# Decode attention with a gated feed-forward branch: other order of loads, other place of the feed-forward part, shorter output sum

## The chip, the cores and the metric

The kernel runs on one core of a Trainium2 chip. The metric is the device time of one execution in microseconds (us), median of several runs. Before the change it is 390.3 us. The profile's span, from the first to the last instruction, is about 1.8 us shorter than the time of the same run.

Engines: PE is the TensorE matrix engine (PEld its weight loads), DVE the VectorE, ACT the ScalarE, POOL the GpSimd, SP the SyncE, which here only issues DMA transfers. SP and POOL each feed a DMA queue of their own: q1 (hardware) is SP's, q0 (software) is POOL's. The trace of the changed kernel shows it: from 30 to 90 us, when only SP's keys are loaded, q1 moves 24.98 of 25.12 MB, and from 156 to 186 us, when only POOL's values are, q0 moves 12.55 of 12.60 MB.

## The reference

Two sequences (B = 2), one new token each, 32 heads of width 128, 4096 cached keys and values per head, everything in bf16:

```python
x = A_x                                                     # [2, 1, 512]
g = sigmoid((x * gate_w).sum(-1, keepdims=True))
q = (x @ wq).reshape(B, 1, 32, 128).transpose(0, 2, 1, 3)
p = softmax(einsum("bhqd,bhkd->bhqk", q, k_cache) * 128 ** -0.5)
o = einsum("bhqk,bhkd->bhqd", p, v_cache)
a = o.transpose(0, 2, 1, 3).reshape(B, 1, 4096) @ wo        # wo: [4096, 512]
b = relu(x @ w1) @ w2                                       # w1: [512, 1376], w2: [1376, 512]
return g * a + (1 - g) * b
```

The caches are read once: 64 keys and 64 values ("K0" to "K63", "V0" to "V63", one per head and sequence) of 1 MiB each. The weights wq and wo are 4 MiB each, w1 and w2 1.4 MB each. By my estimate from the numbers below (146.1 MB at 420 GB/s are 348 of the 387.6 us of the span) it is a kernel that should run at the speed of its loads.

## The kernel before

For each sequence ("batch" in what follows): load the 32 keys, transpose each on TensorE, multiply by the query; then one softmax over all heads; then the 32 values, in groups of four heads; each group's output goes through its part of wo. Keys have four buffers (KN), transposed keys four (KT), values seven (varena). wq, w1 and w2 lie in the memory of the value buffers, so no value can be loaded before the feed-forward part (FFN) is done. The loads are issued like this (cut):

```python
@block.sync
def _(sp):
    for i in range(NHEAD):                                   # the 64 keys
        s, u = kn_slot(i)
        if i == 0:
            sp.wait_ge(d_w2b, 16)                            # all of w2 has landed
        if u > 0:
            sp.wait_ge(pe_tk[NQ - 1], i - NKN + 1)           # the key four earlier is transposed
        sp.dma_start(out=KN[s], in_=...).then_inc(kn_sem[s], 16)
    sp.wait_ge(dv_out, 3)
    sp.dma_start(out=out..., in_=out_bf[0:1, :]).then_inc(d_out, 16)

@block.gpsimd
def _(pool):
    pool.iota(...); pool.iota(...)
    # x, gate_w, wq, w1, w2 (two parts), wo: all issued here, in this order
    pool.wait_ge(pe_f2, 1)                                   # FFN done: the value buffers are free
    for i in range(NHEAD):                                   # the 64 values
        b, h = divmod(i, Hq)
        s, u = vslot(i)
        if h == 0:
            il = b * Hq + Hq - 1                             # the batch's last key has landed
            ks, ku = kn_slot(il)
            pool.wait_ge(kn_sem[ks], 16 * (ku + 1))
        if u > 0:
            pool.wait_ge(vfree[s], u)                        # the head seven earlier is done
        pool.dma_start(out=VS[s], in_=...).then_inc(vsem[s], 16)
```

TensorE does everything in program order: the query projection, the FFN, then per batch the keys (scores two heads behind the transposes), the softmax transposes, the values. The DVE adds each group's output row to `acc_row` and at the very end forms `(acc - b) * g + b` in three operations over 1x1024 elements on one partition.

## Time and profile before

| | before |
|---|---|
| time, median (lowest to highest) | 390.3 us (389.2 to 391.5) |
| span of the profiled run | 387.6 us |
| bytes moved | 146.1 MB |
| rate in undisturbed stages | 418 to 423 GB/s |
| PE busy | 82% of the span |
| key head: transposes and scores on PE / its DMA at 420 GB/s | 1.94 + 0.55 us / 2.50 us |

These lines of the page are the span, the busy share of the DMA engines in 40 slices of 9.7 us, and what they moved in each slice:

```profile
span 387.6 us, 10707 instructions
...
DMA  4999999999999999999992699999978999999950
GB/s 180 419 344 389 409 419 419 418 420 420 419 398 420 422 419 420 419 421 419 420 419 117 220 413 423 419 419 419 421 316 315 427 419 418 420 420 420 419 221 0
```

146.1 MB at 420 GB/s are 348 us. So 40 us of the span are not explained by bytes, and the GB/s line shows where they are: the first slices, slice 3 (344), slices 22 and 23 (117 and 220), slices 30 and 31 (316 and 315), and the last two.

A finer reading is needed to know what ends each hole. The following lines are of the view by windows. The columns are the window, its length, busy time and number of instructions of PE, PEld, DVE, ACT and POOL, then the granted TensorE clock (1.00 is full speed), the busy share of the DMA engines, and GB/s. First the start:

```profile
0.00:4.00 4.00, 0.00 (x0) 0.00 (x0) 1.72 (x4) 1.28 (x1) 3.36 (x9) 1.00 0.01 1
4.00:8.00 4.00, 0.37 (x8) 0.29 (x8) 2.66 (x4) 0.00 (x0) 4.00 (x5) 1.00 0.78 256
```

Then the place between the batches:

```profile
204.00:208.00 4.00, 3.43 (x59) 3.24 (x60) 0.00 (x0) 0.00 (x0) 0.00 (x0) 1.00 0.54 221
208.00:212.00 4.00, 3.50 (x50) 2.47 (x47) 0.75 (x2) 0.00 (x0) 0.00 (x0) 1.00 0.02 8
212.00:216.00 4.00, 4.00 (x49) 2.75 (x49) 3.33 (x7) 0.02 (x1) 0.00 (x0) 1.00 0.02 4
216.00:220.00 4.00, 4.00 (x72) 3.47 (x69) 4.00 (x7) 2.45 (x3) 0.00 (x0) 1.00 0.76 256
```

TensorE works at full clock all the time while DMA moves next to nothing from 208 to 216 us: the values of batch 0 have all landed, four keys of batch 1 were loaded long ago, the fifth key waits for TensorE to transpose the first, and the first value of batch 1 waits for the last key. That wait is in the list of waits (engine, what it was about to do, what it waited for: us in total, times, longest):

```profile
POOL varena L204 <- DMA kn_arena<-in_A_k_cache_dram: 206.9, 2, 110.5
```

and what it costs is seen when it ends for the second time, at 291 us, just after the last key has landed:

```profile
284.00:288.00 4.00, 3.27 (x53) 2.10 (x50) 2.71 (x5) 2.02 (x2) 0.00 (x0) 1.00 0.98 403
288.00:292.00 4.00, 3.25 (x55) 2.73 (x56) 2.04 (x4) 1.01 (x1) 0.72 (x2) 1.00 0.13 55
292.00:296.00 4.00, 2.74 (x45) 1.46 (x42) 2.72 (x4) 1.01 (x1) 2.94 (x6) 1.00 0.83 301
```

Finally the end, from the chain of waits (start, duration, what, how many instructions): the last value's matmuls, the output projection of the last groups, and then four DVE operations (the 0.69 us sum of the last group and the three of 1.22 us) that nothing overlaps:

```profile
376.42 1.95 PE PS L453 x32
...
379.68 1.83 PE PS L437 x8
...
381.53 0.69 DVE acc_row L318
...
382.31 1.22 DVE t_row L322
...
383.56 1.22 DVE t_row L327
...
384.81 1.21 DVE out_bf L330
```

### The profile page before, as it was taken

What the parts mean: (1) busy time and instruction counts of PE and PEld (TensorE: products, weight loads), DVE (VectorE), ACT (ScalarE), POOL (GpSimd) and SP (SyncE); (2) the same over time, 40 slices, a digit from 0 to 9 for tenths busy, and PEclk for the clock granted to TensorE, in tenths of its full rate; (3) what the DMA queues carried; (4) which work ended last, traced back from release to release, by engine and by line L of the source; (5) the groups of instructions that cost most, each with busy time, mean ns of one, the idle gap of its engine ahead of it and who ended that gap; (6) DMA issues with size and microseconds to landing.
All of it is one profiled execution on the core that took longest, in us unless ns stands there. A gap on an engine that the chain in (4) does not pass through costs nothing.

```text
span 387.6 us, 10707 instructions
## 1 busy us (share of the span) xinstructions
PE 318.7 (82%) x5008; PEld 258.3 (67%) x5008; DVE 165.0 (43%) x280; ACT 74.9 (19%) x80; POOL 41.4 (11%) x77
## 2 busy tenths in 40 slices
PE   0355799999896688987888999999984799988873
PEld 0333677777673677776776877777762799877761
DVE  4023477777677100111111877777766102111106
ACT  1001244443344300000000433344433100000000
POOL 7000000000003022221200000000003032222000
PEclk9998899999999599999999999999998599999998
DMA  4999999999999999999992699999978999999950
GB/s 180 419 344 389 409 419 419 418 420 420 419 398 420 422 419 420 419 421 419 420 419 117 220 413 423 419 419 419 421 316 315 427 419 418 420 420 420 419 221 0
DMA packets 20766, 146.11 MB, mean 377 GB/s; under 512 B 2194, under 2 KB 2194, under 8 KB 3827
## 3 DMA queue, kind: packets, MB, share of 16 engines
q0 software_dynamic: 11504, 78.32, 49.5%
q1 hardware_dynamic: 9218, 67.12, 42.2%
q8 instruction: 39, 0.64, 0.7%
q14 instruction: 5, 0.03, 0.0%
HBM read 145.43 MB, written 0.00 MB: 375 GB/s over the span
## 4 chain that ended last, share of the span: by engine, by line
DMA 46%; PE 45%; DVE 3%; issue 2%; ACT 2%; POOL 1%; POOLq 0%; DVEq 0%
DMA varena<-in_A_v_cache_dram 27%; PE PS L381 25%; DMA kn_arena<-in_A_k_cache_dram 15%; PE PS L453 11%; PE PS L398 6%; DMA varena<-in_B_w_dram 5%; PE PS L437 2%; DVE mx L272 1%; DVE mx L271 1%; ACT P L221 1%; ACT P L219 1%; ACT kt_arena L212 1%; PE PS L427 0%; DVE t_row L327 0%; DVE t_row L322 0%
## 5 line engine op out<-in xcount | busy, mean ns | idle before, releaser
L453 PE MATMUL PS<-varena,pT 128*1 128x128 bf16 x2048 | 127.2, 223 | 20.1 <-DMA varena<-in_A_v_cache_dram 17.8
L381 PEld LDWEIGHTS PS<-iden,kn_arena 128*128 128x128 bf16 x2048 | 116.4, 99 | 38.4 <-DMA kn_arena<-in_A_k_cache_dram 36.7
L269 DVE COPY kt_arena<-PS 128x1024 bf16<-128x1024 bf16 x192 | 120.7, 684 | 45.8 <-PE PS L381 45.8
L453 PEld LDWEIGHTS PS<-varena,pT 128*1 128x1 bf16 x2048 | 118.5, 86 | 30.3 <-DMA varena<-in_A_v_cache_dram 25.7
L381 PE MATMUL PS<-iden,kn_arena 128*128 128x128 bf16 x2048 | 127.2, 221 | 9.8 <-DMA kn_arena<-in_A_k_cache_dram 9.6
L212 ACT COPY kt_arena<-PS 128x1024 bf16<-128x1024 bf16 x64 | 64.8, 1012 | 218.6 <-PE PS L381 218.6
L204 POOL DMA_DIRECT2D varena<-in_A_v_cache_dram x64 | 33.9, 532 | 318.7 <-DMA kn_arena<-in_A_k_cache_dram 206.9
L307 DVE TENSOR_TENSOR osb<-PS,rs_row 1x512 bf16<-1x512 f32 x16 | 10.9, 679 | 133.8 <-PE PS L453 133.8
L398 PE MATMUL PS<-kt_arena,Qm 128*32 128x512 bf16 x512 | 39.0, 384 | 0.4 <-ACT kt_arena L212 0.4
L437 PE MATMUL PS<-wo_sb,OT 128*1 128x512 bf16 x64 | 16.1, 378 | 0.0
L398 PEld LDWEIGHTS PS<-kt_arena,Qm 128*32 128x32 bf16 x512 | 8.0, 94 | 8.0 <-DVE kt_arena L269 1.4
L318 DVE TENSOR_TENSOR acc_row<-acc_row,PS 1x512 f32<-1x512 f32 x16 | 10.8, 675 | 5.8 <-PE PS L437 5.8
L346 PE MATMUL PS<-xT,varena 128*128 128x2 bf16 x128 | 3.6, 165 | 11.6 <-DMA varena<-in_A_wq_dram 11.6
L346 PEld LDWEIGHTS PS<-xT,varena 128*128 128x128 bf16 x128 | 3.5, 104 | 11.7 <-DMA varena<-in_A_wq_dram 11.7
L364 PE MATMUL PS<-varena,h1T 128*1 128x512 bf16 (+1 forms) x22 | 6.6, 468 | 4.1 <-DMA varena<-in_B_w_dram 4.1
L437 PEld LDWEIGHTS PS<-wo_sb,OT 128*1 128x1 bf16 x64 | 4.2, 82 | 5.0 <-DVE OT L313 0.4
L364 PEld LDWEIGHTS PS<-varena,h1T 128*1 128x1 bf16 (+1 forms) x22 | 2.1, 98 | 8.1 <-DMA varena<-in_B_w_dram 4.1
L249 DVE CAST QT<-PS 128x64 bf16<-128x64 f32 x1 | 0.2, 225 | 12.7 <-PE PS L346 12.7
L415 PE MATMUL PS<-iden,P 32*128 32x32 bf16 x64 | 0.9, 187 | 5.4 <-ACT P L221 5.4
L262 DVE COPY b_row<-PS 1x1024 f32<-1x1024 f32 x1 | 1.2, 1212 | 9.2 <-PE PS L364 9.2
L406 PE MATMUL PS<-idenf,mx 128*1 128x128 f32 x2 | 0.6, 322 | 5.2 <-DVE mx L272 5.2
L415 PEld LDWEIGHTS PS<-iden,P 32*128 32x128 bf16 x64 | 0.7, 101 | 5.6 <-ACT P L221 5.6
(58 smaller groups left out, 53.4 us busy)
## 6 DMA issues: line engine op xcount, KB each, us to landing
kn_arena<-in_A_k_cache_dram SPq DMA_DIRECT2D x64, 1024.0 KB, 7.9
varena<-in_A_v_cache_dram POOLq DMA_DIRECT2D x64, 1024.0 KB, 15.1
varena<-in_A_wq_dram POOLq DMA_DIRECT2D x1, 4096.0 KB, 12.8
wo_sb<-in_A_wo_dram POOLq DMA_DIRECT2D x1, 4096.0 KB, 41.5
varena<-in_B_w_dram POOLq DMA_DIRECT2D x1, 1376.0 KB, 15.5
varena<-in_B_w_dram POOLq DMA_DIRECT2D x1, 1280.0 KB, 19.9
varena<-in_B_w_dram POOLq DMA_DIRECT2D x1, 96.0 KB, 19.4
x_row<-in_A_x_dram POOLq DMA_DIRECT2D x1, 2.0 KB, 2.2
```

Source lines behind the costliest of these rows:

```text
L204: pool.dma_start(out=VS[s], in_=src).then_inc(vsem[s], 16)
L212: act.copy(out=KT[kt_slot(i)][:, (NQ - 1) * JQ * 128:NQ * JQ * 128], in_=STG[NQ - 1]).then_inc(ac_kq, 1)
L219: act.activation(out=P[0:64, :], in_=PS[0:64, 0:PW], func=ACT.Exp, bias=negm[0:64, :], scale=SCALE, accum_out=ssum[0:64, 0:1]).then_inc(ac ...
L269: dve.tensor_copy(out=KT[kt_slot(i)][:, q * JQ * 128:(q + 1) * JQ * 128], in_=STG[q]).then_inc(dv_kq, 1)
L307: dve.tensor_tensor(out=osb[0:1, g * 512:(g + 1) * 512].rearrange("o (m d) -> o m d", m=4), in0=PS[0:1, g * 512:(g + 1) * 512].rearrange(" ...
L318: dve.tensor_tensor(out=acc_row[0:1, b * D:(b + 1) * D], in0=acc_row[0:1, b * D:(b + 1) * D], in1=PS[0:1, gbank(g2) * 512:(gbank(g2) + 1) ...
L346: mm = pe.matmul(QT_ps[:, 2 * h:2 * h + 2], lhsT=wq_sb[:, k, h * Dh:(h + 1) * Dh], rhs=xT[:, k, :], start=(k == 0), stop=(k == KD - 1))
L364: mm = pe.matmul(PS[0:1, B_COL + b * D:B_COL + (b + 1) * D], lhsT=h1T[0:fw, u, b:b + 1], rhs=w2_sb[0:fw, u, :], start=(u == 0), stop=(u == ...
L381: t = pe.transpose(out=STG[q][:, (j - q * JQ) * 128:(j - q * JQ + 1) * 128], in_=KN[s][:, j * Dh:(j + 1) * Dh], identity=iden[:, :])
L398: mm = pe.matmul(PS[32 * tcol:32 * tcol + 32, beta * 512:(beta + 1) * 512], lhsT=Qm[:, b, h, :], rhs=kt[:, c * 512:(c + 1) * 512], start=( ...
L437: mm = pe.matmul(PS[0:1, gbank(g) * 512:(gbank(g) + 1) * 512], lhsT=OT[:, b, h:h + 1], rhs=wo_sb[:, h, :], start=(m == 0), stop=(m == 3))
L453: mm = pe.matmul(PS[0:1, col:col + Dh], lhsT=pT[:, j, h:h + 1], rhs=VS[s][:, j * Dh:(j + 1) * Dh], start=(j == 0), stop=(j == NJ - 1))
```

## The change

The intent is to keep DMA busy where it ran dry, and to shorten the end:

1. w1 and w2 get memory of their own (paid for by three KT buffers instead of four and by placing small rows in memory that is free at that time), so values get eight buffers and need not wait for the FFN.
2. SP issues half of wq and then w1 and w2 at the very start; POOL issues the other half of wq before x. Keys wait for wq only.
3. The FFN moves on TensorE and DVE from before the first key to between the softmax and the values of batch 0.
4. wo is loaded after the keys of batch 0, by SP instead of POOL, and K32 and the keys after it are held back until V30 has landed.
5. The values of a batch start when its third key from the end has landed.
6. `(1 - g) * b` is put into `acc_row` once; each group's row is then added as `g * row + acc` in one fused operation, and the last one writes the output.

```diff
-    NKT = 4
-    NADDR_V = 7
+    NKT = 3
+    NADDR_V = 8
+    w1_sb = sb("w1_sb", [128, KD, Dff], BF16)        # were parts of varena
+    w2_sb = sb("w2_sb", [128, NFF, D], BF16)
...
     @block.sync
+        # wq rows of the second half -> d_wq2, then w1, then w2 (two parts)
         for i in range(NHEAD):
+            if b > 0 and h == 0:
+                sp.dma_start(out=wo_sb[:, :, :], in_=A_wo.rearrange("(h p) n -> p h n", p=128)).then_inc(d_wo, 16)
+                vs_, vu_ = vslot(b * Hq - 2)
+                sp.wait_ge(vsem[vs_], 16 * (vu_ + 1))
             if i == 0:
-                sp.wait_ge(d_w2b, 16)
+                sp.wait_ge(d_wq, 16)
+                sp.wait_ge(d_wq2, 16)
...
     @block.gpsimd
-        # x, gate_w, wq, w1, w2, wo
-        pool.wait_ge(pe_f2, 1)
+        # first half of wq, x, gate_w
+        pool.wait_ge(pe_q, 1)
...
-                il = b * Hq + Hq - 1
+                il = b * Hq + Hq - 3
...
     @block.vector
-                    dve.tensor_tensor(out=acc_row[...], in0=acc_row[...], in1=PS[...], op=ALU.add)
-        # t1 = acc - b;  t1 = t1 * g;  out = t1 + b     (1x1024 each)
+                    dst = acc_row if g2 < NG - 1 else out_bf
+                    dve.scalar_tensor_tensor(out=dst[...], in0=PS[...], scalar=g_row[0:1, b:b + 1],
+                                             in1=acc_row[...], op0=ALU.mult, op1=ALU.add)
...
     @block.tensor
-        # query projection, FFN, then the batches
+        # query projection, then the batches; in batch 0 the FFN follows the softmax transposes,
+        # and the values wait until its result is copied out (dv_bcp)
```

## The prediction

> **What bounds it now.** The DMA queues view gives 146.1 MB. In undisturbed stages the windows view shows 418 to 423 GB/s at a DMA share of 1.01, so the bytes alone need about 348 us of the 387.6 us span. A key head takes TensorE 1.94 + 0.55 = 2.49 us in the chain of waits and DMA 1.05 MB / 420 = 2.50 us: balanced. A value head takes TensorE about 2.0 us. The kernel is bound by DMA, and its 40 us above the byte time are holes (windows of 2 us):
> - start: nothing until about 5.4 us; POOL issues everything;
> - 18 to 44 us: 320 to 410 GB/s, about 3 us lost;
> - 205 to 219 us: about 11.5 us lost between the batches. Only four keys of batch 1 are prefetched; the next waits for TensorE, values for the last key;
> - 287 to 293.5 us: about 5 us lost, because batch 1's first value waits until the last key has landed (POOL idle 96 us, ended at 291.3);
> - from the last value's bytes (about 375 us) to the end: 12.6 us, with four DVE operations after the last matmul (0.68 and three of 1.21 us).
>
> **What the change does.** Bytes and matmuls stay the same.
> - SP issues half of wq and the FFN weights at once; I expect data from about 2.2 us: 3 us gained. Keys wait for wq only; the first lands at about 23.5 us instead of 34. Most of that is no gain: wo's 4.2 MB (10 us) only moves to the values of batch 0.
> - K32 to K35 move from early in the values of batch 0 to its end, where DMA was empty; wo takes their old place. The 11.5 us hole shrinks to about 1 us: 10 us gained, the largest term.
> - Values start two keys earlier: the 5 us hole almost closes (4 to 4.5 us), though the last two keys, sharing the engines, land about 2.5 us later.
> - Tail: three 1.21 us operations with gaps (3.8 us) go; the fused one should cost the same 0.68 us.
> - Cost: the FFN (1.6 us + relu + 6.6 us + copy, about 11 us with gaps) now stands between softmax and values of batch 0, partly at the half clock that the trace shows there (0.50). The eighth value slot and wo give DMA 35 us of queued work from the 30th key on, TensorE's pause is about 33 us: 0 to 3 us of new hole.
> - Cost: the first keys meet a half clock (3.6 instead of 1.96 us) with only keys to load: up to 2 us of hole.
>
> [...]
>
> **Sum.** Span 387.6 - 3 - 10 - 4.5 - 3.8 + 2 = 368, less about 2 of the early dip: 366; with the 1.8 us between span and time, 368 us, 5.7% faster. Range 362 to 376. Faster by over 2%: 0.95; within: 0.04; slower: 0.01.
>
> **What would show it.** DMA share near 1.0 through both batch changes; first key transposed near 23.5 us; batch 1's first transpose near 198 us (214 now); one short DVE operation after the last output matmul.
>
> **What would make it wrong.** A hole of over 4 us behind the FFN; keys sharing with values so that the key chain falls behind; TensorE, nearly as long as DMA, becoming the bound.

## The result

| | before | changed |
|---|---|---|
| time, median (lowest to highest, runs) | 390.25 us (389.15 to 391.5, 16) | 370.37 us (369.46 to 372.04, 9) |
| ratio, 95% interval | | 0.950 (0.948 to 0.951) |
| span of the profiled run | 387.6 us | 368.5 us |
| first transpose of a key | 34.3 us | 23.6 us |
| first transpose of batch 1 | 214.0 us | 201.5 us |
| packets of all DMA | 20,766 | 25,133 |

Ratios in this document are the mean time of one kernel's runs over that of the other's of the same rounds, so they are not quite the ratio of the medians. Executions over 1.5% slower than the fastest of the same kernel are left out of the means. The kernel is 5.0% faster.

The same lines of the page, for the changed kernel (a slice is 9.2 us):

```profile
span 368.5 us, 10705 instructions
...
DMA  8999999999999999999998999999999999999990
GB/s 304 397 399 421 422 416 421 419 417 420 397 407 408 392 393 415 419 420 423 416 383 317 421 422 414 420 422 420 419 414 414 419 349 419 422 420 419 421 393 10
```

The DMA line now has a 9 or an 8 in all but the last slice. The GB/s line is the more honest one: slices 11 to 15 (392 to 408), 21 and 22 (383 and 317) and 33 (349) still show losses, some of them under a 9.

The same windows, the start, then the place between the batches, then the second softmax:

```profile
0.00:4.00 4.00, 0.00 (x0) 0.00 (x0) 0.96 (x3) 1.28 (x1) 3.33 (x9) 1.00 0.55 152
4.00:8.00 4.00, 0.00 (x0) 0.00 (x0) 0.00 (x0) 0.00 (x0) 0.00 (x0) 1.00 1.00 422
```

```profile
190.00:194.00 4.00, 3.42 (x59) 3.04 (x55) 0.46 (x1) 0.00 (x0) 0.00 (x0) 1.00 0.74 307
194.00:198.00 4.00, 3.45 (x59) 3.26 (x60) 0.00 (x0) 0.00 (x0) 0.00 (x0) 1.00 0.79 297
198.00:202.00 4.00, 4.00 (x37) 1.90 (x35) 2.68 (x6) 0.00 (x0) 0.00 (x0) 1.00 0.98 336
```

```profile
274.00:278.00 4.00, 4.00 (x67) 2.90 (x65) 2.83 (x6) 2.02 (x2) 3.10 (x6) 1.00 0.98 391
278.00:282.00 4.00, 3.41 (x60) 2.81 (x57) 2.79 (x5) 1.01 (x1) 1.07 (x3) 1.00 1.01 418
296.00:300.00 4.00, 4.00 (x71) 4.00 (x69) 0.00 (x0) 0.00 (x0) 1.06 (x2) 0.95 0.81 299
300.00:304.00 4.00, 4.00 (x76) 4.00 (x73) 0.68 (x1) 0.00 (x0) 1.41 (x3) 1.00 1.02 375
```

And the end of the chain of waits: one fused operation stands after the last matmul (L457 is the output projection, L343 the fused sum).

```profile
361.04 1.95 PE PS L475 x32
...
364.30 1.83 PE PS L457 x8
...
366.16 0.74 DVE Qm L343
```

### A ledger of lost DMA time

To compare the two kernels stage by stage, take windows of 2 us and count in each how much time its bytes did not need at 420 GB/s: 2 us minus GB/s times 2 us over 420. The sum over the span is the span minus 348 us, so every microsecond of difference between the two spans must be in one of the lines. (A stage at a rate slightly over 420 gives a small negative number.)

| stage | before | changed | difference |
|---|---|---|---|
| start, to 18 / 16 us | 5.5 | 2.7 | -2.8 |
| rest of the weights, first keys, to 44 / 24 us | 2.8 | 0.8 | -2.0 |
| rest of the keys of batch 0 | 0.6 | 0.2 | -0.4 |
| values of batch 0 (from 120 / 96 us) | 0.0 | 2.3 | +2.4 |
| between the batches (204 to 220 / 190 to 200) | 11.3 | 3.0 | -8.4 |
| keys of batch 1 | 0.4 | 0.2 | -0.2 |
| around the second softmax (286 to 294 / 274 to 306) | 4.8 | 1.8 | -3.0 |
| values of batch 1 | -0.1 | -0.1 | 0.0 |
| end (from 372 / 358 us) | 14.3 | 9.7 | -4.6 |
| total | 39.7 | 20.5 | -19.1 |

The total is the difference of the spans, 387.6 - 368.5. The largest line is the one that the prediction had as its largest. One line has the wrong sign: the values of batch 0 lose 2.3 us that they did not lose before. (The last keys of batch 0 fall into that stage in the changed kernel.) A ledger says where time was lost, not that undoing one cause would bring it back; that is what the experiments are for.

### The profile page after: what moved, and what is told of

Its sections match the earlier page's. It is cut to its first block, busy times and chain, and to the rows that moved or that the text cites. A ratio compares the mean times of both kernels' runs of the same rounds, so it can differ in the third digit from the quotient of the medians.

```text
span 368.5 us, 10705 instructions
## 1 busy us (share of the span) xinstructions
PE 314.0 (85%) x5008; PEld 255.8 (69%) x5008; DVE 162.9 (44%) x278; ACT 75.0 (20%) x80; POOL 37.2 (10%) x73
## 2 busy tenths in 40 slices
DMA packets 25133, 146.11 MB, mean 397 GB/s; under 512 B 2209, under 2 KB 7681, under 8 KB 8194
## 4 chain that ended last, share of the span: by engine, by line
PE 51%; DMA 41%; DVE 3%; ACT 2%; issue 2%; SPq 1%; POOL 0%; another core or an unknown queue 0%; POOLq 0%
PE PS L401 24%; DMA varena<-in_A_v_cache_dram 19%; DMA kn_arena<-in_A_k_cache_dram 19%; PE PS L475 17%; PE PS L416 6%; DMA varena<-in_A_wq_dram 3%; PE PS L384 2%; PE PS L457 1%; DVE mx L294 1%; DVE mx L293 1%; ACT P L229 1%; SPq L187 1%; ACT P L227 1%; ACT kt_arena L220 1%; PE PS L374 0%
## 5 line engine op out<-in xcount | busy, mean ns | idle before, releaser
L475 PE MATMUL PS<-varena,pT 128*1 128x128 bf16 x2048 | 122.0, 221 | 12.6 <-DMA varena<-in_A_v_cache_dram 9.9
L475 PEld LDWEIGHTS PS<-varena,pT 128*1 128x1 bf16 x2048 | 116.2, 85 | 20.0 <-DMA varena<-in_A_v_cache_dram 14.3
L331 DVE TENSOR_TENSOR kt_arena<-PS,rs_row 1x512 bf16<-1x512 f32 x16 | 10.9, 678 | 119.1 <-PE PS L475 119.1
L457 PE MATMUL PS<-wo_sb,OT 128*1 128x512 bf16 x64 | 16.1, 378 | 0.8 <-DMA wo_sb<-in_A_wo_dram 0.8
L343 DVE SCALAR_TENSOR_TENSOR acc_row<-PS,g_row,acc_row 1x512 f32<-1x512 f32 x14 | 10.3, 738 | 6.2 <-PE PS L457 6.2
L355 PE MATMUL PS<-iden,x_row 1*128 1x1 bf16 x8 | 0.4, 163 | 14.8 <-DMA x_row<-in_A_x_dram 14.8
L355 PEld LDWEIGHTS PS<-iden,x_row 1*128 1x128 bf16 x8 | 0.3, 101 | 14.8 <-DMA x_row<-in_A_x_dram 14.8
L457 PEld LDWEIGHTS PS<-wo_sb,OT 128*1 128x1 bf16 x64 | 4.2, 82 | 5.9 <-DVE OT L337 1.4
L384 PE MATMUL PS<-w_sb,h1T 128*1 128x512 bf16 (+1 forms) x22 | 7.6, 523 | 0.4 <-DVE h1T L271 0.4
L247 DVE TENSOR_TENSOR t_row<-x_row,gw_row 1x1024 f32<-1x1024 bf16 x1 | 1.2, 1211 | 12.0 <-DMA gw_row<-in_gate_w_dram 12.0
L384 PEld LDWEIGHTS PS<-w_sb,h1T 128*1 128x1 bf16 (+1 forms) x22 | 2.3, 107 | 5.3 <-issue 4.4
## 6 DMA issues: line engine op xcount, KB each, us to landing
wo_sb<-in_A_wo_dram SPq DMA_DIRECT2D x1, 4096.0 KB, 52.7
w_sb<-in_B_w_dram SPq DMA_DIRECT2D x1, 1280.0 KB, 19.1
```

Of the source, the lines that this page charges most:

```text
L331: dve.tensor_tensor(out=osb[0:1, g * 512:(g + 1) * 512].rearrange("o (m d) -> o m d", m=4), in0=PS[0:1, g * 512:(g + 1) * 512].rearrange(" ...
L343: dve.scalar_tensor_tensor(out=dst[0:1, b * D:(b + 1) * D], in0=PS[0:1, gbank(g2) * 512:(gbank(g2) + 1) * 512], scalar=g_row[0:1, b:b + 1] ...
L384: mm = pe.matmul(PS[0:1, B_COL + b * D:B_COL + (b + 1) * D], lhsT=h1T[0:fw, u, b:b + 1], rhs=w2_sb[0:fw, u, :], start=(u == 0), stop=(u == ...
L457: mm = pe.matmul(PS[0:1, gbank(g) * 512:(gbank(g) + 1) * 512], lhsT=OT[:, b, h:h + 1], rhs=wo_sb[:, h, :], start=(m == 0), stop=(m == 3))
L475: mm = pe.matmul(PS[0:1, col:col + Dh], lhsT=pT[:, j, h:h + 1], rhs=VS[s][:, j * Dh:(j + 1) * Dh], start=(j == 0), stop=(j == NJ - 1))
```

## The experiments

All give correct outputs. "Cost" is the difference of the ratios to the kernel before, times 390 us, because each group of runs had its own runs of the kernel before beside it. The intervals of the single ratios reach 0.2 to 0.6% to each side, so a cost under 2 us is not settled by the times alone; there I lean on the ledger of the profiled run.

| run | what differs | median us | ratio | cost against the changed kernel |
|---|---|---|---|---|
| k_early | keys of batch 1 not held back | 379.61 | 0.9708 | +8.3 |
| v_last | values wait for the last key again | 374.75 | 0.9585 | +3.5 |
| tail_old | old output sum | 375.70 | 0.9601 | +4.1 |
| ffn_front | FFN before the keys again | 386.29 | 0.9877 | +14.9 |
| pool_start | POOL issues the first loads again | 373.39 | 0.9566 | +2.7 |
| v_seven | seven value buffers | 371.35 | 0.9517 | +0.8 |
| wo_wide | wo in runs of 4 KB | 368.49 | 0.9448 | -1.9 |
| ffn_front_wide | FFN in front, wo in runs of 4 KB | 374.88 (3 fast runs) | 0.9594 | +3.8 |
| ffn_front_wide_again | the same kernel, other runs | 373.13 | 0.9559 | +2.5 |
| hold3 | wo_wide, keys held until V29 | 368.57 | 0.9452 | -1.7 |
| tail_early | wo_wide, earlier output matmuls | 367.70 | 0.9434 | -2.4 |
| best | wo_wide, hold3, tail_early, nine value buffers | 367.28 | 0.9415 | -3.2 |

### One part undone at a time

My theory was that the gain is the filled holes plus the shorter end. A rival was that TensorE is nearly as long as DMA in this kernel (314 us busy), so that the order of the loads hardly matters and the gain comes from taking the FFN out of the way of the first keys.

**k_early.** The keys of batch 1 follow wo at once.

```diff
-                vs_, vu_ = vslot(b * Hq - 2)
-                sp.wait_ge(vsem[vs_], 16 * (vu_ + 1))
```

> The changed kernel, but K32 to K35 are not held back until value 30 has landed; they follow wo at once, as far as buffers are free. Theory (filling the hole between the batches is the largest term): DMA runs dry again between the last value of batch 0 and TensorE's first transposes of batch 1, some 8 to 10 us of empty DMA, and the time rises from 370.4 to 378 to 380 us. Rival (the gain came from taking the FFN out of the way of the first keys, and TensorE is as long as DMA anyway, so the order of keys and values hardly matters): at most 373 us.

Measured: 379.61 us. The windows between the batches show the hole as it was in the kernel before:

```profile
206.00:210.00 4.00, 3.49 (x46) 2.50 (x47) 1.12 (x3) 0.00 (x0) 0.00 (x0) 1.00 0.00 0
210.00:214.00 4.00, 4.00 (x53) 2.89 (x52) 3.55 (x7) 0.48 (x1) 0.00 (x0) 1.00 0.02 4
```

The ledger has 12.0 us there (200 to 220 us) against 3.0 us, a difference of 9.0 us, and the times say 8.3. So the place between the batches is worth 8 to 9 us, and it is the holding back of four keys that fills it: the same 4 MB moved at a time when nothing else can be loaded. The rival falls here.

**v_last.** The values wait for the last key.

```diff
-                il = b * Hq + Hq - 3
+                il = b * Hq + Hq - 1
```

> The changed kernel, but the values of a batch wait for its last key again, not for the third from the end. Theory: the hole of about 5 us before the values of batch 1 comes back; batch 0 has wo to load there and shows no hole; time up by 4 to 4.5 us, to about 374.5. Rival (the values that start early take bandwidth from the last two keys, TensorE's softmax starts later, and most of the gain is given back): up by less than 2 us.

Measured: 374.75 us, a cost of 3.5 us by ratio. The hole before the values of batch 1 is back (ledger around the second softmax 4.7 us against 1.8):

```profile
276.00:280.00 4.00, 3.94 (x65) 2.75 (x63) 2.92 (x5) 2.02 (x2) 0.20 (x1) 1.00 0.22 86
```

The prediction's worry that early values delay the last two keys by 2.5 us did not come true. In the changed kernel's timeline the last key's transposes start 3.1 us after those of the key before in batch 1 and 2.8 us in batch 0, where 2.5 us is the normal distance: a delay of 0.6 and 0.3 us.

**tail_old.** The output sum from zero and the three operations of 1x1024 after it, as in the kernel before.

```diff
-                    dve.scalar_tensor_tensor(out=dst[...], in0=PS[...], scalar=g_row[0:1, b:b + 1], in1=acc_row[...], ...)
+                    dve.tensor_tensor(out=acc_row[...], in0=acc_row[...], in1=PS[...], op=ALU.add)
+        # after the loop: t1 = acc - b;  t1 = t1 * g;  out = t1 + b
```

> The changed kernel, but the output is combined as before: a sum from zero, then three operations of 1x1024 after the last matmul. Theory: nothing hides the tail, so all of the three operations with their gaps, 3.7 to 3.8 us, comes back: about 374.1 us. Rival: none that I believe in; less than 3 us would mean that the fused operation costs more than it replaced.

Measured: 375.70 us, by ratio 4.1 us, with an interval of 2 us to each side; the ledger's last stage is 13.3 us against 9.7, that is 3.6 us. This agrees with the 3.7 us that the three operations take in the chain of the kernel before. The fused operation takes 0.74 us where the plain sum took 0.68. The ledger of the two original kernels has 4.6 us here, one more than the operations explain: before, the last value but one kept TensorE waiting 2.1 us (at 374 us), afterwards 0.5 us. Why those last transfers drained differently I have not found out.

**pool_start.** POOL issues x, the gate, wq, w1 and w2 behind its iotas, as before; SP issues only keys and wo.

```diff
     @block.sync
-        # second half of wq, w1, w2
     @block.gpsimd
-        # first half of wq, x, gate_w
+        # x, gate_w, wq, w1, w2
```

> The changed kernel, but POOL issues x, the gate, wq, w1 and w2 again, in the old order, behind its two iotas. Theory: the first bytes move 2.8 us later (1.43 MB against 0.24 MB moved by 6 us), and all of it is on the path: 373 us. Rival (the earlier small loads let the query projection start sooner and make up for it): 371 us or less.

Measured: 373.39 us, 2.7 us by ratio; the ledger's start is 5.5 us against 2.7. The interval of the times is 2 us to each side, but both numbers say that all of the earlier start is on the path. The page gives a check on the packets that matter below: with w2 back on POOL's queue, there are 1,376 fewer packets of 512 B to 2 KB than in the changed kernel, one for each row of w2.

**v_seven.** One value buffer less.

```diff
-    NADDR_V = 8
+    NADDR_V = 7
```

> The changed kernel with seven value slots instead of eight. Theory: the pause of TensorE at the second softmax ends after DMA has filled the eight slots (242 GB/s at 296 to 298 us), so one slot less adds one value's DMA time, 2.5 us, there; batch 0 has wo to fill its pause and should add nothing, or at most 1 us: 372.5 to 373.5 us. Rival (eight slots are not needed): within 1 us of 370.4.

Measured: 371.35 us, 0.8 us by ratio: less than I expected. The hole is there. This is the window just after the softmax of batch 1, first of the changed kernel, then with seven buffers:

```profile
294.00:298.00 4.00, 4.00 (x54) 4.00 (x52) 0.00 (x0) 0.00 (x0) 0.53 (x1) 0.70 0.89 334
```

```profile
294.00:298.00 4.00, 4.00 (x62) 4.00 (x61) 0.00 (x0) 0.00 (x0) 1.03 (x2) 0.82 0.37 115
```

The ledger has 4.2 us around the second softmax instead of 1.8, as expected, but 0.6 us less between the batches and 0.6 us less at the end, so that the spans differ by 1.2 us only. That these small gains belong to the seventh buffer and not to the scatter of single profiles is not shown.

### The feed-forward part, and a load that starved

**ffn_front.** The FFN stands before the first scores again, with the early weights and their own buffers kept.

```diff
         q_pe()
+        ffn_pe()
         for b in range(B):
...                                       # in batch 0, after the softmax transposes
-            if b == 0:
-                ffn_pe()
...                                       # first scores share banks with the FFN result
-                if b > 0:
+                if b == 0:
+                    pe.wait_ge(dv_bcp, 1)
+                else:
                     pe.wait_ge(dv_acc, 1 + b * NG)
```

> The changed kernel, but the FFN stands between the query projection and the first scores again, with its own weight buffers and early weight loads kept. Theory: the first transposes start 8 to 9 us later (about 32 us instead of 23.6), the four key buffers fill meanwhile and DMA runs dry for about 6 us; batch 0's pause before the values is shorter, which gains nothing because DMA had work queued there: 375 to 377 us. Rival (where the FFN stands doesn't matter, the values loaded ahead pay it back): 371 us.

Measured: 386.29 us. This is 10 us more than my own theory said, and the rival is further off still. The front is as expected: with the four key buffers full, DMA waits for TensorE (5.4 us in the ledger from 24 to 40 us):

```profile
30.00:34.00 4.00, 3.90 (x42) 2.40 (x40) 1.95 (x3) 0.06 (x1) 0.00 (x0) 1.00 0.06 23
```

But there is a second hole of 11.1 us, from 160 to 186 us, that I had not foreseen. TensorE stops dead in the middle of the values, and the list of waits names the reason:

```profile
PE PS L460 <- DMA wo_sb<-in_A_wo_dram: 23.9, 1, 23.9
```

```profile
168.00:172.00 4.00, 1.18 (x3) 0.37 (x4) 0.00 (x0) 0.00 (x0) 0.00 (x0) 0.50 0.21 74
172.00:176.00 4.00, 4.00 (x35) 3.65 (x34) 0.74 (x1) 0.00 (x0) 0.00 (x0) 0.50 0.00 0
```

TensorE has finished twelve value heads and wants the first output matmul; wo has not landed. It took 70.4 us from issue to landing, for 4 MB that need 10 us at 420 GB/s. While TensorE waits, no value buffer comes free; DMA fills the eight buffers, has nothing left but the rest of wo, and from 170 us on, with wo landed too, it is idle until TensorE frees the next buffer.

```profile
wo_sb<-in_A_wo_dram SPq DMA_DIRECT2D x1, 4096.0 KB, 70.4
```

Why so slow? Look at the DMA queues of the changed kernel itself, from 112 to 126 us, while wo (q1) and values (q0) are both under way. The columns are packets, MB, and the time that the packets took as a share of 16 engines' time:

```profile
q0 software_dynamic: 680, 5.02, 86.9%
q1 hardware_dynamic: 679, 0.70, 14.8%
```

In this stretch the two queues move the same number of packets, 680 and 679, and a value's packet is seven times as large (7.4 KB against 1.0 KB). wo's rows are 1 KB each, and 0.70 MB in 679 packets are about one row to a packet. The counts are as close in ffn_front: 786 against 787 from 124 to 140 us and 796 against 795 from 148 to 164 us. So in the changed kernel's stretch wo gets 0.70 of 5.73 MB, an eighth of the bytes. Why the counts are equal there is not shown. In the kernel before, the same rows were issued by POOL, and there they travelled in larger packets: from 36 to 46 us wo moved 1.09 MB in 282 packets, 3.9 KB each. The page's count says the same for the whole run; the first line is of the kernel before, the second of the changed one:

```profile
DMA packets 20766, 146.11 MB, mean 377 GB/s; under 512 B 2194, under 2 KB 2194, under 8 KB 3827
```

```profile
DMA packets 25133, 146.11 MB, mean 397 GB/s; under 512 B 2209, under 2 KB 7681, under 8 KB 8194
```

The packets of 512 B to 2 KB went from none to 5,472, which is the number of rows of wo (4,096) and w2 (1,376).

Then in the changed kernel wo got through only because of the FFN's place: TensorE's pause of 10.9 us before the values leaves the eight value buffers full, POOL has nothing to issue, and from 126 to 134 us wo has most of the engines' time (2.11 of 2.92 MB). It landed at 148.7 us, 52.7 us after its issue, and TensorE waited 0.8 us for it. That was luck, not design. v_seven shows it from the other side: with seven buffers the values queued ahead are through earlier, from 124 to 130 us wo has the engines almost alone (1.96 of 2.09 MB, at 348 GB/s together), and the same 1 KB rows land after 37.8 us. So the time to landing depends on how long the values compete, not on the rows alone. The lines are of the changed kernel and of v_seven (KB, us from issue to landing):

```profile
wo_sb<-in_A_wo_dram SPq DMA_DIRECT2D x1, 4096.0 KB, 52.7
```

```profile
wo_sb<-in_A_wo_dram SPq DMA_DIRECT2D x1, 4096.0 KB, 37.8
```

This makes a forecast: if the rows were larger, the stall should go, and the 2.3 us that the values of batch 0 lose in the changed kernel should go too.

**wo_wide.** Each partition takes four neighbouring rows of wo in one run of 4 KB; the transposes of the output row read every fourth element, so that the products are the same.

```diff
-                sp.dma_start(out=wo_sb[:, :, :], in_=A_wo.rearrange("(h p) n -> p h n", p=128))
+                sp.dma_start(out=wo_sb[:, :, :].rearrange("p (g m) n -> p g (m n)", m=4),
+                             in_=A_wo.rearrange("(g p m) n -> p g (m n)", p=128, m=4))
...
-                t = pe.transpose(out=ots[...], in_=osb[0:1, h * Dh:(h + 1) * Dh], ...)
+                t = pe.transpose(out=ots[...], in_=osb[0:1, g * 512 + m:(g + 1) * 512:4], ...)
```

> The changed kernel, with wo loaded in runs of 4 KB (four neighbouring rows to a partition, and the output transposes reading every fourth element to match) instead of 1 KB. Theory: on the SP queue each 1 KB row is a packet of its own (679 packets of 0.70 MB beside 680 packets of 5.02 MB of values from 112 to 126 us), so wo gets an eighth of the bytes beside values; with 4 KB rows it gets about a third, lands some 20 us sooner than 52.7 us after its issue, and DMA no longer falls to about 350 GB/s at 126 to 132 us. Gain 1 to 3 us: about 368.5 us. Rival (it only takes bandwidth from the values, and a lower GB/s at a full DMA share was no loss): 370 to 371 us.

Measured: 368.49 us, 1.9 us by ratio, which the times alone do not settle. wo lands 36.2 us after its issue instead of 52.7, nobody waits for it, and from 112 to 126 us it now has a third of the bytes:

```profile
wo_sb<-in_A_wo_dram SPq DMA_DIRECT2D x1, 4096.0 KB, 36.2
```

```profile
q0 software_dynamic: 528, 3.84, 66.1%
q1 hardware_dynamic: 488, 1.97, 35.0%
```

The packet counts of the two queues are near each other again (528 against 488). The stage from 96 to 136 us loses 0.5 us instead of 2.2. The loss was of a kind that the busy share hides. These are the windows from 128 to 130 us, of the changed kernel and of this one: at a share of 1.10 the engines moved 351 GB/s, at 1.01 they move 420. In the second window wo is nearly through (0.04 of 0.84 MB), so this is not the rate of 4 KB packets. That comes from the queue lines: from 112 to 126 us, wo's 0.70 MB in 14.8% of the engines' time are 338 GB/s in 1 KB packets, and 1.97 MB in 35.0% are 402 in 4 KB packets.

```profile
128.00:130.00 2.00, 2.00 (x40) 2.00 (x37) 0.00 (x0) 0.00 (x0) 0.54 (x2) 1.00 1.10 351
```

```profile
128.00:130.00 2.00, 2.00 (x40) 2.00 (x37) 0.00 (x0) 0.00 (x0) 0.58 (x2) 1.00 1.01 420
```

**ffn_front_wide.** Both edits together.

> The kernel with the FFN in front, and wo loaded in runs of 4 KB. Theory: the FFN in front cost 16 us because of two things, about 5 to 6 us of empty DMA before the fifth key and about 10 us from wo landing 70 us after its issue, for which TensorE waited 23.9 us. The second goes: about 376 us. Rival (the stall is due to the order of the keys, the values and wo, not to the size of the rows): still over 383 us.

Measured: three runs of 373.24 to 375.57 us, close to the 376 expected and far from the rival's 383, and one of 530.57 us. The profile fell into that one: its granted clock was 0.577 in the mean, and TensorE was busy for 93% of the span at little more than half speed. Nothing is concluded from it. I ran the kernel again for a profile.

**ffn_front_wide_again.**

> The same kernel as the run with the FFN in front and wide wo rows, whose profile fell in a state with a clock of 0.58. Theory: 374 to 376 us again, wo lands under 40 us after its issue and TensorE does not wait for it; the hole before the fifth key, about 5 us, stays.

Measured: 373.13 us, 0.9 us below the range that I had given. wo lands in 36.0 us, TensorE does not wait for it, and the ledger has 4.7 us from 24 to 40 us and nothing from 136 to 186 us. So the FFN in front had two costs: 11 to 12 us for the starved load (0.9877 less 0.9594 and 0.9559, times 390 us) and 4 to 6 us for the place itself (the latter two less wo_wide's 0.9448).

### Further

**hold3.** On wo_wide, K32 is released one value earlier.

```diff
-                vs_, vu_ = vslot(b * Hq - 2)
+                vs_, vu_ = vslot(b * Hq - 3)
```

> The kernel with wide wo rows (368.5 us), with K32 to K35 released when value 29 has landed instead of value 30. In the changed kernel about 3 us of DMA time are lost at 190 to 200 us, because the keys are issued at 194.0, when the last value's bytes are nearly through. Theory: one value earlier closes most of that and delays the last value by about 1 us: gain 1 to 2 us. Rival: the keys take bandwidth from the last two values, TensorE finishes batch 0 later, and the fifth key with it: no gain, or up to 1 us slower.

Measured: 368.57 us against 368.49, no gain; the rival was right. The ledger between the batches is 3.5 us instead of 2.9. The hole has only moved: the four keys are issued sooner, at 189.5 us instead of 192.1, and then DMA waits at 202 to 206 us for TensorE, which has to finish batch 0 before it frees the first key buffer. It finishes later, as the rival said: TensorE waits 1.77 us for the last value instead of 0.52, and the first transposes of batch 1 start at 200.8 us instead of 199.7.

```profile
202.00:206.00 4.00, 4.00 (x75) 3.98 (x73) 4.00 (x8) 2.02 (x2) 0.00 (x0) 1.00 0.65 223
```

**tail_early.** On wo_wide, the outputs of the sixth and seventh group are projected between the last four heads.

```diff
                     mm.then_inc(vfree[s], 1)
+                    if g == NG - 1 and m == 0:
+                        ot_transposes(b, g - 1); wo_partial(b, g - 2)
+                    if g == NG - 1 and m == 1:
+                        wo_partial(b, g - 1)
...
             ot_transposes(b, NG - 1)
-            wo_partial(b, NG - 2)
             wo_partial(b, NG - 1)
```

(The DVE's order in the last group changes with it: it copies the seventh group's transposed output before it waits for the eighth.)

> The kernel with wide wo rows, with the output matmuls of the sixth and seventh group done between the last four value heads, where TensorE waits for DMA anyway, instead of after the last. Theory: after the last value's matmuls there remain one evacuation, four transposes, a copy, four output matmuls and the fused sum: 1 us less at the end, about 367.5 us. Rival: the last value waits for these matmuls: no gain.

Measured: 367.70 us, 0.5 us better than wo_wide by ratio, with intervals that overlap and one of its six runs at 370.66 us: a gain is likely and not settled.

**best.** wo_wide, hold3 and tail_early, and nine value buffers; the ninth fits when the scratch row of the gate lies in wo's memory, which is loaded later.

> Wide wo rows, the release after value 29, the early output matmuls, and a ninth value slot (the scratch row for the gate's products lies in wo's buffer, which is loaded later). Theory: the gains add, and the ninth slot closes the hole of 1.6 us at the second softmax: 364 to 366 us. Rival: the ninth value only delays the last two keys as it did between seven and eight slots: 366 to 367 us.

Measured: 367.28 us (367.13 to 367.70), ratio 0.9415 with an interval of 0.9396 to 0.9434. It is the fastest of all kernels here by its median (its interval overlaps tail_early's), and 3.2 us faster than the changed one, but slower than both the theory (364 to 366) and the rival (366 to 367) said: the gains did not add. The ninth buffer does what it should: around the second softmax the ledger has 0.05 us.

```profile
294.00:298.00 4.00, 4.00 (x67) 4.00 (x65) 0.00 (x0) 0.00 (x0) 0.84 (x2) 0.89 1.01 420
```

Yet the end grows from wo_wide's 9.3 to 10.4 us, because DMA is now done before TensorE. From 286 us to the end TensorE waits 2.2 us in all for values (4.0 us in the changed kernel, 6.7 us before), and in the last windows DMA has run out while TensorE works without a gap:

```profile
354.00:356.00 2.00, 2.00 (x34) 1.86 (x33) 0.74 (x1) 0.00 (x0) 0.00 (x0) 1.00 0.51 209
356.00:358.00 2.00, 2.00 (x29) 1.47 (x26) 0.00 (x0) 0.00 (x0) 0.00 (x0) 1.00 0.11 37
```

The bound has changed engine at the end of the kernel. A further gain at this end would have to come from TensorE's work on the values, not from loads; no run here tries it. Earlier in the kernel, the ledger still has 2.6 us at the start and 2.9 us between the batches.

## Why the prediction was right

The time predicted was 368 us, within 362 to 376; it was 370.4. That it came so close is partly luck: the two largest terms were 1 to 1.6 us too large each, the tail came out about 1 us larger than the cause named for it, and the 2 us set down for costs were lost to something else. Point by point:

- **Bound and sum.** The kernel was bound by DMA, and the gain is holes filled: the ledger's difference is 19.1 us of lost DMA time, at unchanged bytes. This step holds. The costs of the parts undone singly do not add up to it: k_early, v_last, tail_old and pool_start come to 18.6 us and the FFN's place to another 4 to 6, against 19.7 us gained by ratio. A part undone in the changed kernel meets other neighbours than in the kernel before; how much of the difference that explains is not shown.
- **Start, 3 us.** 2.8 us in the ledger, 2.7 us by pool_start. The first key was transposed at 23.6 us; 23.5 had been predicted.
- **Early dip, about 2 us.** 2.0 us.
- **"The 11.5 us hole shrinks to about 1 us: 10 us gained."** The mechanism is right (k_early gives 8.3 us back), the size was too large: 3.0 us remain and 8.4 us were gained. The release comes with a landing: SP issued the keys at 194.0 us, when the values' bytes were nearly through, and DMA ran at 225 and 160 GB/s from 192 to 196 us. hold3 shows that an earlier release doesn't help, since TensorE's end of batch 0 then leaves the hole a little later.
- **"The 5 us hole almost closes (4 to 4.5 us)."** It closed, but the ledger gained 3.0 us and v_last 3.5, because a new hole of about 1.6 us opened after the softmax, when the eight value buffers were full (best closes it with a ninth). The delay of 2.5 us for the last two keys was mis-sized: 0.3 and 0.6 us.
- **Tail, 3.8 us.** 3.6 us in tail_old's ledger and 4.1 us by its times; 4.6 us between the two original kernels, of which about 1 us has no cause that I have shown.
- **FFN, "0 to 3 us of new hole".** The pause was 10.9 us (11 predicted) and made no hole. 2.2 us were lost there all the same, but to wo's small packets, which wo_wide takes away. The number was right for a wrong reason.
- **First keys at half clock, "up to 2 us".** One key took 3.44 us, the next ones 1.96, but the granted clock reads 1.00 in each window of 2 us from 22 to 30 us, so a half clock is not shown there; the ledger has 0.2 us from 24 to 96 us.
- **Batch 1's first transpose "near 198 us".** It was at 201.5 us, 3.5 us late. The 2.2 us lost to small packets lie before it; the rest I have not traced.

What the prediction missed altogether is that "wo takes their old place" is not an exchange of equal bytes. It weighed loads by size only. That wo nearly arrived too late was not in its list of what could go wrong, and it was a near thing: ffn_front, with the same load order and a shorter pause, lost 11 us to it.

On the clock, the traces show a granted clock of 0.50 around and after both softmaxes in both kernels (126 to 134 and 300 to 308 us before, 114 to 122 and 288 to 296 us in the changed kernel), and in ffn_front, whose stall began at 147 us, 0.81 from 148 to 150 us and 0.50 from 150 us to the end of the stall at 171 us. TensorE had been idle or nearly so just before in each case. What lowers the clock is not shown: it reads 1.00 in the changed kernel from 4 to 14 us too, where TensorE does nothing.

## What to carry to other kernels

In a kernel bound by loads, write down for each stage what the load queues have to do and which wait gives them their next work; move a load that nothing else depends on into the stage where they run dry, and check the result with a ledger of lost bytes, since a busy share near 1 can hide slow small packets (here a share of 1.10 at 351 GB/s). When two queues share the engines, compare their packet sizes, not only their bytes: here a load with 1 KB rows on SP's queue got an eighth of the bytes beside one with 8 KB rows (0.70 of 5.73 MB from 112 to 126 us), and arrived in time only because another stage happened to pause. Once the holes are closed, look for the engine that is now last before adding more buffers.

## Packet sizes, rates and one slow execution, as measured

- SP's queue moved wo's 1 KB rows at about one row to a packet (679 packets for 0.70 MB from 112 to 126 us of the changed kernel), while POOL's queue moved the same tensor at 3.9 KB per packet (282 for 1.09 MB from 36 to 46 us of the kernel before). Beside values in packets of 7.4 KB, and with eight value buffers, a 4 MB load in 1 KB rows took 52.7 us to land (changed kernel) and 70.4 us (ffn_front); in 4 KB runs, with the same edits otherwise, it took 36.2 us (wo_wide) and 36.0 us (ffn_front_wide_again).
- Almost alone from 124 to 130 us in v_seven, the 1 KB rows ran at about 348 GB/s, and in the shared stretch from 112 to 126 us of the changed kernel at 338 GB/s of their own time, against 402 in 4 KB runs (wo_wide, the same stretch) and 420 of undisturbed stages.
- One execution of ffn_front_wide, on one core, had a mean granted clock of 0.577 and took 530.57 us, against 374.88 us in the median of its three fast runs. Its cause is open.
